# Straight writes and even-odd reads of PSUM in an induced attention and maxout kernel

## The chip, the cores and the metric

The kernel runs on one core of a Trainium2 chip. The metric is the device time of one execution in microseconds (us). The engines that matter are TensorE (PE in the profile, with its weight loads as PEld), ScalarE (ACT), VectorE (DVE) and GpSimd (POOL); SyncE (SP) issues nearly all DMAs. SBUF is the on-chip working memory, PSUM the memory that matmuls write; it has eight banks of 512 fp32 columns on each of 128 partitions.

## What is computed

```python
def mab(q, kv):
    s = scale * (q @ kv.transpose(0, 2, 1))
    s = s - s.max(-1, keepdims=True)
    a = np.exp(s)
    a /= a.sum(-1, keepdims=True) + 1e-09
    return a @ kv
h = mab(I, x)          # x: 4 x 12544 x 128, I: 32 inducing points per batch
x = mab(x, h)          # every token attends to the 32 rows of h
h = np.maximum(np.maximum(x @ w1, x @ w2), x @ w3)     # 128 -> 768
out = h @ w_out                                        # 768 -> 128
```

All is in fp32 to the accuracy of a split: a value is kept as a high part, rounded to the type fp32r in which a matmul runs at one pass, and a low part that holds the rest.

## The kernel before

A batch has 12544 tokens, cut into one narrow group of 256 tokens and six groups of 2048. A full group is worked in four chunks of 512 tokens; the narrow one is one chunk of 256. So a batch has 25 chunks and the whole has 100. Each chunk goes through six slots (`NJ = 6`, 128 of the 768 hidden columns each), 600 slots in all.

For a token the second attention gives 32 weights. The weights' high and low halves, each twice, fill the 128 rows of a tile `pT`, and the columns of `pT` are the chunk's tokens. The matrix `us` holds w1-w2, w3-w2 and a product through `w_out`, each already multiplied with the batch's attended points. With z = x w2 the maximum of three is z + max(relu(x(w1-w2)), x(w3-w2)), and z's own way through `w_out` is folded into the third part of `us`.

A slot does this, in `advance()` and, `LAG = 6` slots later, in `stage2()`:

- PE: a product into bank `pu` (line 787) and one into bank `pv` (line 797), both reading `pT`. There are two banks of each.
- ACT: `ru` = relu of `pu`, from PSUM to SBUF (line 806).
- DVE: `h` = maximum of `pv` in PSUM and `ru` in SBUF (line 827).
- ACT: `hi` = `h` rounded to fp32r (line 816), SBUF to SBUF.
- POOL, in some slots DVE: `lows` = `h` - `hi` (lines 824 and 830).
- PE: three products that add into bank `acc`: `wo_hi` with `hi`, `wo_lo` with `hi`, `wo_hi` with `lows` (lines 863 to 865). In a chunk's first slot a fourth goes ahead of them, the third part of `us` with `pT` (line 862).

After a chunk's sixth slot `finish()` copies `acc` to `o` in SBUF (line 876, on ACT but for the first three chunks and a half of the last) and stores it.

Once in a group of 24 slots `scores_steps()` makes the weights: products (line 692), transposes, exponentials and divisions in a PSUM bank `aux`, then ACT writes the high halves `ph` (line 739) and DVE the low halves `pl` (line 742). SP's DMAs move them row by row into the `pT` of four chunks (line 768), two chunks ahead of their use. The first attention of the next batch (lines 366 to 545) is put in between as single steps until the last batch, where nothing follows.

The order of everything is written out by hand: the slot loop in `main()` and a table of slots. Each engine does its list in that order.

A matmul's moving operand is not read column by column here. `woven` reads the two halves of 512 columns in turn: 0, 256, 1, 257 and so on. So the output's columns come in another order than the input's. Before the change this is made up for in SBUF: `ph` and `pl` are written scattered (`spread`), value 4b+2d+a of a row at column 256d+128a+b, so that each written value is 128 or more columns from the last. `pu`, `pv`, `ru`, `h`, `hi` and `lows` then hold the chunk in an order that a second reading by halves puts right, and `acc` and `o` come out straight. The product of line 862 makes one step where the others make two, so it reads `pT` by quarters in turn: 0, 128, 256, 384, 1 and so on. The narrow chunks (`full` is false) are read and written straight throughout.

```python
    def woven(ap, full):
        return ap.rearrange("p (a b) -> p b a", a=2) if full else ap
    def spread(ap, full):
        return ap.rearrange("p (d a b) -> p b d a", d=2, a=2) if full else ap
```

Of the kernel before, what the change touches and what calls it, by code (L numbers as in the profile page):

```python
# [8 lines left out]
F32 = mybir.dt.float32  # L9
# [3 lines left out]
AF = mybir.ActivationFunctionType  # L13
# [12 lines left out]
def kernel(ctx, tc, x, xt, ind_t, w1, w2, w3, w_out, out):  # L26
    nc = tc.nc
    B, N, C = x.shape
    M = ind_t.shape[1]
    DF = w1.shape[1]  # L30
    P = 128
    NT = N // P
    NJ = DF // P
# [158 lines left out]
    def first_load(what):  # L192
# [12 lines left out]
        out=sel[:, :M], in_=ident.rearrange("p (q m) -> p m q", m=M), axis=AX.X, op=ALU.add  # L205
    )
    nc.vector.tensor_copy(
        out=sel[:, M:].rearrange("p (q m) -> p q m", m=M),
        in_=sel[:, :M].unsqueeze(1).to_broadcast([P, NQ - 1, M]),
# [17 lines left out]
    wo_hi = const.tile([P, NJ, C], F32R, name="wo_hi")  # L227
    wo_lo = const.tile([P, NJ, C], F32R, name="wo_lo")
# [54 lines left out]
    def row_of(j):  # L283

        return 2 * (j % (NJ // 2)) + j // (NJ // 2)
# [388 lines left out]

    def woven(ap, full):

        return ap.rearrange("p (a b) -> p b a", a=2) if full else ap

    def spread(ap, full):

        return ap.rearrange("p (d a b) -> p b d a", d=2, a=2) if full else ap

    def scores_products(b, gi, bank):
        nt = groups[gi]["nt"]
# [10 lines left out]
    def scores_steps(b, gi):  # L697

        nt = groups[gi]["nt"]
        w = nt * M  # L700
        st = state[b]
        sp = st["s"].pop(gi)
        flat = sp[:, :w]
        ev = flat.rearrange("p (t m) -> p t m", m=M)
        nc.vector.transpose(out=flat, in_=flat)
        yield
        mx = wk.tile([P, GT], F32, name="mx", tag="mx")
        nc.vector.tensor_reduce(out=mx[:, :nt], in_=ev, axis=AX.X, op=ALU.max)
        yield
        nc.vector.tensor_sub(out=ev, in0=ev, in1=mx[:, :nt].unsqueeze(2).to_broadcast([P, nt, M]))  # L710
        yield
        nc.scalar.activation(out=flat, in_=flat, func=AF.Exp, scale=scale)
        yield
        rs = wk.tile([P, GT], F32, name="rs", tag="rs")
        nc.vector.tensor_reduce(out=rs[:, :nt], in_=ev, axis=AX.X, op=ALU.add)
        yield
        if b == 0 and gi < 2:
            nc.vector.tensor_scalar_add(out=rs[:, :nt], in0=rs[:, :nt], scalar1=1e-9)
        else:
            nc.scalar.activation(out=rs[:, :nt], in_=rs[:, :nt], func=AF.Identity, bias=eps)  # L720
        yield
        nc.vector.reciprocal(out=rs[:, :nt], in_=rs[:, :nt])
        nc.vector.tensor_mul(out=ev, in0=ev, in1=rs[:, :nt].unsqueeze(2).to_broadcast([P, nt, M]))
        yield
        if nt < GT:

            pn = wk.tile([P, nt, 2, 2, M], F32R, name="pn", tag="pn", bufs=1)
            e4 = ev.unsqueeze(2).to_broadcast([P, nt, 2, M])
            nc.scalar.copy(out=pn[:, :, :, 0, :], in_=e4)
            yield  # L730
            nc.vector.tensor_sub(out=pn[:, :, :, 1, :], in0=e4, in1=pn.bitcast(F32)[:, :, :, 0, :])
            st[("p", gi)] = pn
            yield
            return
        nc.vector.transpose(out=flat, in_=flat)  # L735
        yield
        e4 = flat.rearrange("p (b d a) -> p b d a", d=2, a=2)
        ph = wk.tile([P, 512], F32R, name="ph", tag="ph")
        nc.scalar.copy(out=spread(ph, True), in_=e4)  # L739
        yield  # L740
        pl = wk.tile([P, 512], F32R, name="pl", tag="pl")
        nc.vector.tensor_sub(out=spread(pl, True), in0=e4, in1=spread(ph.bitcast(F32), True))  # L742
        st[("p", gi)] = (ph.bitcast(F32), pl.bitcast(F32))
        yield

# [28 lines left out]
    relus, sums = {}, {}  # L774
# [5 lines left out]
    def advance():  # L780

        s = pipe["next"]
        pipe["next"] += 1
        if s + 1 < len(slots):
            c, j = slots[s + 1]
            pu, w = bank_u[(s + 1) % 2], c.w
            nc.tensor.matmul(  # L787
                out=pu[:, :w],
                lhsT=state[c.b]["us"][:, 2 * j * P : (2 * j + 1) * P],
                rhs=woven(c.pT[:, :w], c.full),  # L790
                start=True,
                stop=True,
            )
        if 0 <= s < len(slots):
            d, j = slots[s]
            pv = bank_v[s % 2]
            nc.tensor.matmul(  # L797
                out=pv[:, : d.w],
                lhsT=state[d.b]["us"][:, (2 * j + 1) * P : (2 * j + 2) * P],
                rhs=woven(d.pT[:, : d.w], d.full),  # L800
                start=True,
                stop=True,
            )
        if s + 1 < len(slots):
            ru = hp.tile([P, 512], F32, name="ru", tag="ru", bufs=3)
            nc.scalar.activation(out=ru[:, :w], in_=pu[:, :w], func=AF.Relu)  # L806
            relus[s + 1] = ru
        low = pipe.pop("low", None)
        if 0 <= s - 1 < len(slots):
            c, j = slots[s - 1]  # L810
            h = sums.pop(s - 1)
            hi = hp.tile([P, 512], F32R, name="hi", tag="hi", bufs=10)
            if s - 1 in HIVEC:
                nc.vector.tensor_copy(out=hi[:, : c.w], in_=h[:, : c.w])
            else:
                nc.scalar.copy(out=hi[:, : c.w], in_=h[:, : c.w])  # L816
            lo = lows[:, (s - 1) % NL, :]
            c.hh.append(hi)
            c.hl.append(lo)
            args = dict(out=lo[:, : c.w], in0=h[:, : c.w], in1=hi.bitcast(F32)[:, : c.w])  # L820
            if c.low(j):
                pipe["low"] = args
            else:
                nc.gpsimd.tensor_sub(**args)  # L824
        if 0 <= s < len(slots):
            h = hp.tile([P, 512], F32, name="h", tag="h", bufs=5)
            nc.vector.tensor_max(out=h[:, : d.w], in0=pv[:, : d.w], in1=relus.pop(s)[:, : d.w])  # L827
            sums[s] = h
        if low:
            nc.vector.tensor_sub(**low)  # L830

    class Chunk:


        def __init__(self, n, b, gi, q):
            self.n, self.b, self.gi, self.q = n, b, gi, q
            self.w = GT * M if q is not None else groups[gi]["nt"] * P
            self.full = q is not None
            self.hh, self.hl = [], []

        def low(self, k):
# [7 lines left out]
    def stage2(c, j):  # L849
        us = state[c.b]["us"]  # L850
        w = c.w
        hi, lo = (woven(t[:, :w], c.full) for t in (c.hh[j], c.hl[j]))
        if j == 0:
            c.acc = [(bank_o[c.n % 2], slice(0, w))]
            if c.n == len(chunks) - 1:
                c.acc = [(bank_a[k], slice(k * w // 2, (k + 1) * w // 2)) for k in range(2)]
        for acc, cs in c.acc:
            to = acc[:, : cs.stop - cs.start]
            two, four = (slice(cs.start // k, cs.stop // k) if c.full else cs for k in (2, 4))
            if j == 0:  # L860
                pT = spread(c.pT[:, :w], c.full)
                nc.tensor.matmul(out=to, lhsT=us[:, 2 * DF :], rhs=pT[:, four], start=True, stop=False)  # L862
            nc.tensor.matmul(out=to, lhsT=wo_hi[:, row_of(j), :], rhs=hi[:, two], start=False, stop=False)  # L863
            nc.tensor.matmul(out=to, lhsT=wo_lo[:, row_of(j), :], rhs=hi[:, two], start=False, stop=False)  # L864
            nc.tensor.matmul(out=to, lhsT=wo_hi[:, row_of(j), :], rhs=lo[:, two], start=False, stop=(j == NJ - 1))  # L865

    def finish(c):
        at = groups[c.gi]["at"] + (c.q or 0) * c.w
        turns = [(nc.vector.tensor_copy if c.n < 3 else nc.scalar.copy, nc.sync)]
        if len(c.acc) > 1:  # L870

            turns = [(nc.vector.tensor_copy, nc.sync), (nc.scalar.copy, nc.scalar)]
        for (acc, cs), (copy, queue) in zip(c.acc, turns):
            o = op.tile([P, 512], F32, name="o", tag="o", bufs=3)
            w = cs.stop - cs.start
            copy(out=o[:, :w], in_=acc[:, :w])  # L876
            queue.dma_start(out=out[c.b, :, at + cs.start : at + cs.stop], in_=o[:, :w])


# [7 lines left out]
    for b in range(B):  # L887
        for gi in range(NG):
            full = groups[gi]["nt"] == GT
# [41 lines left out]
    def begins(win):  # L931
        b, g = divmod(win - 1, NG - 1)
        return b * per_batch + short + g * WIN

    for win, slot, kind, n, gi in MOVES:
        s = begins(win) + slot
# [39 lines left out]
    for n, turns in enumerate(TURNS, start=1):  # L976
        for gi, win, slot, wait, past in turns:
            s = begins(win) + slot
# [9 lines left out]
        s = begins(win) + (8 if slot < 8 else 20)  # L988
# [164 lines left out]
```

## Time and profile before

| What | us |
|---|---|
| median of 3 runs | 800.47 (800.38 to 800.72) |
| the profiled execution | 799.86 |
| its span, first to last instruction | 798.1 |
| PE busy | 781.7 (98%) |
| ACT busy | 737.0 (92%) |
| DVE busy | 641.4 (80%) |
| POOL busy | 638.3 (80%) |

The first relu starts at 47 us; what lies ahead of it loads the inputs and runs the first batch's first attention. From there to 790 us the slots run. The granted TensorE clock is full (1.00) in every stretch. The busy time of PE is modelled, since matmuls overlap; how fast it really goes is read from the distance between the starts of one matmul and the next in the timeline. The same goes for ACT and DVE, where an instruction's record overlaps the next one's by some 0.1 to 0.3 us. The chain is the work that ended last, followed back from the end; a shorter instruction off the chain moves nothing by itself.

### The profile page before, as it was taken

What the parts mean: (1) busy time and instruction counts of PE and PEld (TensorE: products, weight loads), DVE (VectorE), ACT (ScalarE), POOL (GpSimd) and SP (SyncE); (2) the same over time, 40 slices, a digit from 0 to 9 for tenths busy, and PEclk for the clock granted to TensorE, in tenths of its full rate; (3) what the DMA queues carried; (4) which work ended last, traced back from release to release, by engine and by line L of the source; (5) the groups of instructions that cost most, each with busy time, mean ns of one, the idle gap of its engine ahead of it and who ended that gap; (6) DMA issues with size and microseconds to landing.
All of it is one profiled execution on the core that took longest, in us unless ns stands there. A gap on an engine that the chain in (4) does not pass through costs nothing.

```text
span 798.1 us, 14349 instructions
## 1 busy us (share of the span) xinstructions
PE 781.7 (98%) x4567; PEld 627.2 (79%) x4567; DVE 641.4 (80%) x1071; ACT 737.0 (92%) x1529; POOL 638.3 (80%) x523
## 2 busy tenths in 40 slices
PE   8999999999999999999999999999999999999998
PEld 6668878778788787787778877878878788787887
DVE  5898978778877787887886878878888788888875
ACT  5789899899998898998998999999999999999996
POOL 1379868878788797786887978878878888888887
PEclk9999999999999999999999999999999999999999
DMA  9844325274542643543644336334223222222221
GB/s 358 297 132 126 107 79 175 61 247 159 190 138 65 194 132 100 185 119 106 223 132 129 108 103 198 114 112 132 68 82 93 74 80 80 67 84 65 77 81 53
DMA packets 52266, 102.24 MB, mean 128 GB/s; under 512 B 18144, under 2 KB 21344, under 8 KB 46944
## 3 DMA queue, kind: packets, MB, share of 16 engines
q1 hardware_dynamic: 52048, 101.21, 40.3%
q8 instruction: 36, 0.59, 0.3%
q14 instruction: 38, 0.31, 0.1%
q10 hardware_dynamic: 144, 0.13, 0.0%
HBM read 48.12 MB, written 25.69 MB: 92 GB/s over the span
## 4 chain that ended last, share of the span: by engine, by line
ACT 44%; PE 43%; DMA 4%; POOL 3%; DVE 3%; issue 2%; SPq 1%; POOLq 0%; ACTq 0%; DVEq 0%
ACT ru L806 18%; ACT hi L816 18%; PE pu L787 7%; PE acc L863 7%; PE pv L797 7%; PE acc L864 6%; PE acc L865 6%; POOL lows L824 3%; ACT o L876 3%; PE aux L692 3%; DMA raw<-in_w_out_dram 2%; PE acc L502 2%; ACT ph L739 2%; PE aux L366 2%; PE acc L862 1%
## 5 line engine op out<-in xcount | busy, mean ns | idle before, releaser
L824 POOL TENSOR_TENSOR lows<-h,hi 128x512 fp32r<-128x512 f32 (+1 forms) x504 | 623.1, 1268 | 123.6 <-ACT hi L816 120.0
L827 DVE TENSOR_TENSOR h<-pv,ru 128x512 f32<-128x512 f32 (+1 forms) x600 | 400.5, 674 | 122.6 <-PE pv L797 57.1
L806 ACT ACTIVATE ru<-pu 128x512 f32<-128x512 f32 (+1 forms) x600 | 402.0, 671 | 36.9 <-PE pu L787 36.7
L816 ACT CAST hi<-h 128x512 fp32r<-128x512 f32 (+1 forms) x596 | 410.9, 690 | 0.8 <-DVE h L827 0.6
L787 PE MATMUL pu<-pT,us 128*128 128x512 f32 (+1 forms) x600 | 229.6, 383 | 6.5 <-ACT ru L806 5.9
L797 PE MATMUL pv<-pT,us 128*128 128x512 f32 (+1 forms) x600 | 226.3, 377 | 1.7 <-DVE h L827 1.6
L863 PE MATMUL acc<-hi,wo_hi 128*128 128x512 f32 (+1 forms) x594 | 225.9, 380 | 0.0
L865 PE MATMUL acc<-lows,wo_hi 128*128 128x512 f32 (+1 forms) x594 | 222.8, 375 | 0.0
L864 PE MATMUL acc<-hi,wo_lo 128*128 128x512 f32 (+1 forms) x594 | 222.8, 375 | 0.0
L787 PEld LDWEIGHTS pu<-pT,us 128*128 128x128 f32 x600 | 113.1, 188 | 40.3 <-ACT ru L806 22.7
L863 PEld LDWEIGHTS acc<-hi,wo_hi 128*128 128x128 f32 x594 | 112.2, 189 | 22.1 <-issue 7.5
L797 PEld LDWEIGHTS pv<-pT,us 128*128 128x128 f32 x600 | 113.3, 189 | 20.0 <-DVE h L827 5.2
L864 PEld LDWEIGHTS acc<-hi,wo_lo 128*128 128x128 f32 x594 | 112.4, 189 | 20.2
L865 PEld LDWEIGHTS acc<-lows,wo_hi 128*128 128x128 f32 x594 | 112.2, 189 | 15.3
L830 DVE TENSOR_TENSOR lows<-h,hi 128x512 fp32r<-128x512 f32 x96 | 80.6, 839 | 0.8 <-ACT hi L816 0.8
L876 ACT COPY o<-acc 128x512 f32<-128x512 f32 (+1 forms) x96 | 64.5, 672 | 0.0
L862 PE MATMUL acc<-pT,us 128*128 128x512 f32 (+1 forms) x99 | 43.0, 434 | 0.0
L742 DVE TENSOR_TENSOR pl<-aux,ph 128x512 fp32r<-128x512 f32 x24 | 25.9, 1078 | 13.5 <-ACT ph L739 13.5
L739 ACT CAST ph<-aux 128x512 fp32r<-128x512 f32 x24 | 28.1, 1171 | 0.2 <-DVE aux L735 0.2
L502 PEld LDWEIGHTS acc<-xg,aT 128*32 128x32 f32 x640 | 18.0, 110 | 9.7 <-issue 8.0
L692 PE MATMUL aux<-xT,hT 128*32 128x512 f32 x192 | 25.1, 603 | 0.0
L366 PE MATMUL aux<-xT,iT 128*32 128x512 f32 x184 | 24.1, 596 | 0.2 <-ACT pT L765 0.2
(163 smaller groups left out, 450.9 us busy)
## 6 DMA issues: line engine op xcount, KB each, us to landing
out_dram<-o SPq DMA_DIRECT2D x95, 256.0 KB, 2.2
xg<-in_x_dram SPq DMA_DIRECT2D x23, 1024.0 KB, 5.9
xT<-in_xt_dram SPq DMA_DIRECT2D x18, 1024.0 KB, 5.5
pT<-ph SPq DMA_DIRECT2D x190, 64.0 KB, 2.0
pT<-pl SPq DMA_DIRECT2D x190, 64.0 KB, 2.0
raw<-in_w_dram SPq DMA_DIRECT2D x3, 768.0 KB, 8.6
us<-uh SPq DMA_DIRECT2D x24, 52.0 KB, 1.9
us<-ul SPq DMA_DIRECT2D x24, 52.0 KB, 2.6
```

The source lines that it names most:

```text
L787: nc.tensor.matmul(out=pu[:, :w], lhsT=state[c.b]["us"][:, 2 * j * P : (2 * j + 1) * P], rhs=woven(c.pT[:, :w], c.full), start=True, stop= ...
L797: nc.tensor.matmul(out=pv[:, : d.w], lhsT=state[d.b]["us"][:, (2 * j + 1) * P : (2 * j + 2) * P], rhs=woven(d.pT[:, : d.w], d.full), start ...
L806: nc.scalar.activation(out=ru[:, :w], in_=pu[:, :w], func=AF.Relu)
L816: nc.scalar.copy(out=hi[:, : c.w], in_=h[:, : c.w])
L824: nc.gpsimd.tensor_sub(**args)
L827: nc.vector.tensor_max(out=h[:, : d.w], in0=pv[:, : d.w], in1=relus.pop(s)[:, : d.w])
L830: nc.vector.tensor_sub(**low)
L862: nc.tensor.matmul(out=to, lhsT=us[:, 2 * DF :], rhs=pT[:, four], start=True, stop=False)
L863: nc.tensor.matmul(out=to, lhsT=wo_hi[:, row_of(j), :], rhs=hi[:, two], start=False, stop=False)
L864: nc.tensor.matmul(out=to, lhsT=wo_lo[:, row_of(j), :], rhs=hi[:, two], start=False, stop=False)
L865: nc.tensor.matmul(out=to, lhsT=wo_hi[:, row_of(j), :], rhs=lo[:, two], start=False, stop=(j == NJ - 1))
L876: copy(out=o[:, :w], in_=acc[:, :w])
```

## The change

The scattered writes go and the reads of PSUM take their place.

- Every product of `pT`, `hi` and `lows`, that of line 862 and those of the narrow chunks too, reads halves in turn (`turned`).
- `ph` and `pl` are written straight.
- A product's output in PSUM then holds token 256a+b at column 2b+a. The relu, the maximum and the output copy read their PSUM bank by even columns first and odd columns after (`sorted_`, every second fp32, twice 256 of them) and write straight (`halves` only gives the straight side the same shape). `ru`, `h`, `hi`, `lows` and `o` are all in the tokens' order.

Each engine has the same instructions in the same order as before; only access patterns differ.

```diff
-    def woven(ap, full):
-        return ap.rearrange("p (a b) -> p b a", a=2) if full else ap
-    def spread(ap, full):
-        return ap.rearrange("p (d a b) -> p b d a", d=2, a=2) if full else ap
+    def turned(ap):
+        return ap.rearrange("p (a b) -> p b a", a=2)
+    def sorted_(ap):
+        return ap.rearrange("p (b a) -> p a b", a=2)
+    def halves(ap):
+        return ap.rearrange("p (a b) -> p a b", a=2)
...
-        e4 = flat.rearrange("p (b d a) -> p b d a", d=2, a=2)
         ph = wk.tile([P, 512], F32R, name="ph", tag="ph")
-        nc.scalar.copy(out=spread(ph, True), in_=e4)
+        nc.scalar.copy(out=ph, in_=flat)
         yield
         pl = wk.tile([P, 512], F32R, name="pl", tag="pl")
-        nc.vector.tensor_sub(out=spread(pl, True), in0=e4, in1=spread(ph.bitcast(F32), True))
+        nc.vector.tensor_sub(out=pl, in0=flat, in1=ph.bitcast(F32))
...
-                rhs=woven(c.pT[:, :w], c.full),
+                rhs=turned(c.pT[:, :w]),
...
-                rhs=woven(d.pT[:, : d.w], d.full),
+                rhs=turned(d.pT[:, : d.w]),
...
-            nc.scalar.activation(out=ru[:, :w], in_=pu[:, :w], func=AF.Relu)
+            nc.scalar.activation(out=halves(ru[:, :w]), in_=sorted_(pu[:, :w]), func=AF.Relu)
...
-            nc.vector.tensor_max(out=h[:, : d.w], in0=pv[:, : d.w], in1=relus.pop(s)[:, : d.w])
+            nc.vector.tensor_max(out=halves(h[:, : d.w]), in0=sorted_(pv[:, : d.w]), in1=halves(relus.pop(s)[:, : d.w]))
...
-        hi, lo = (woven(t[:, :w], c.full) for t in (c.hh[j], c.hl[j]))
...
-                pT = spread(c.pT[:, :w], c.full)
-                nc.tensor.matmul(out=to, lhsT=us[:, 2 * DF :], rhs=pT[:, four], start=True, stop=False)
-            nc.tensor.matmul(out=to, lhsT=wo_hi[:, row_of(j), :], rhs=hi[:, two], start=False, stop=False)
-            nc.tensor.matmul(out=to, lhsT=wo_lo[:, row_of(j), :], rhs=hi[:, two], start=False, stop=False)
-            nc.tensor.matmul(out=to, lhsT=wo_hi[:, row_of(j), :], rhs=lo[:, two], start=False, stop=(j == NJ - 1))
+                nc.tensor.matmul(out=to, lhsT=us[:, 2 * DF :], rhs=turned(c.pT[:, cs]), start=True, stop=False)
+            nc.tensor.matmul(out=to, lhsT=wo_hi[:, row_of(j), :], rhs=turned(c.hh[j][:, cs]), start=False, stop=False)
+            nc.tensor.matmul(out=to, lhsT=wo_lo[:, row_of(j), :], rhs=turned(c.hh[j][:, cs]), start=False, stop=False)
+            nc.tensor.matmul(out=to, lhsT=wo_hi[:, row_of(j), :], rhs=turned(c.hl[j][:, cs]), start=False, stop=(j == NJ - 1))
...
-            copy(out=o[:, :w], in_=acc[:, :w])
+            copy(out=halves(o[:, :w]), in_=sorted_(acc[:, :w]))
```

## Rows read from the trace of the kernel before

**Rows 1.** The page: busy time, share of the span and instructions of each engine.

```profile
PE 781.7 (98%) x4567; PEld 627.2 (79%) x4567; DVE 641.4 (80%) x1071; ACT 737.0 (92%) x1529; POOL 638.3 (80%) x523
```

**Rows 2.** Busy time by stretch: start, end, length, then PE, PEld, DVE, ACT, POOL.

```profile
0.00:48.00 48.00, 43.24 (x468) 29.61 (x469) 34.96 (x72) 33.28 (x79) 15.17 (x19) 1.00 0.85 316
...
442.00:562.00 120.00, 118.10 (x666) 94.38 (x666) 96.95 (x156) 112.89 (x231) 98.55 (x79) 1.00 0.43 131
...
772.00:798.00 26.00, 22.78 (x122) 20.03 (x120) 16.36 (x22) 19.73 (x39) 21.39 (x16) 1.00 0.18 61
```

**Rows 3.** The page: the chain that ended last, by engine and by line.

```profile
ACT 44%; PE 43%; DMA 4%; POOL 3%; DVE 3%; issue 2%; SPq 1%; POOLq 0%; ACTq 0%; DVEq 0%
ACT ru L806 18%; ACT hi L816 18%; PE pu L787 7%; PE acc L863 7%; PE pv L797 7%; PE acc L864 6%; PE acc L865 6%; POOL lows L824 3%; ACT o L876 3%; PE aux L692 3%; DMA raw<-in_w_out_dram 2%; PE acc L502 2%; ACT ph L739 2%; PE aux L366 2%; PE acc L862 1%
```

**Rows 4.** Timeline of ACT, two pieces: start, length, instruction.

```profile
385.56 0.72 ACT L816 CAST hi<-h 128x512 fp32r<-128x512 f32 x1
386.07 1.19 ACT L739 CAST ph<-aux 128x512 fp32r<-128x512 f32 x1
386.94 0.74 ACT L806 ACTIVATE ru<-pu 128x512 f32<-128x512 f32 x1
387.47 0.72 ACT L816 CAST hi<-h 128x512 fp32r<-128x512 f32 x1
...
390.96 0.73 ACT L876 COPY o<-acc 128x512 f32<-128x512 f32 x1
391.44 0.75 ACT L806 ACTIVATE ru<-pu 128x512 f32<-128x512 f32 x1
```

**Rows 5.** Timeline of PE beside it; idle time and its releaser in brackets.

```profile
387.05 0.38 PE L865 MATMUL acc<-lows,wo_hi 128*128 128x512 f32 x1
387.74 0.48 PE L787 MATMUL pu<-pT,us 128*128 128x512 f32 x1 [0.31 <-ACT ru L806]
...
389.14 0.38 PE L797 MATMUL pv<-pT,us 128*128 128x512 f32 x1
389.36 0.44 PE L862 MATMUL acc<-pT,us 128*128 128x512 f32 x1
389.63 0.38 PE L863 MATMUL acc<-hi,wo_hi 128*128 128x512 f32 x1
```

**Rows 6.** Timeline of PE, two products of a narrow chunk and the next.

```profile
236.46 0.28 PE L787 MATMUL pu<-pT,us 128*128 128x256 f32 x1
236.58 0.28 PE L797 MATMUL pv<-pT,us 128*128 128x256 f32 x1
236.70 0.44 PE L862 MATMUL acc<-pT,us 128*128 128x512 f32 x1
```

**Rows 7.** Instruction groups, shapes apart: count, busy us, mean ns, idle before.

```profile
L806 ACT ACTIVATE ru<-pu 128x512 f32<-128x512 f32 x576 | 391.8, 680 | 36.3 <-PE pu L787 36.1
L876 ACT COPY o<-acc 128x512 f32<-128x512 f32 x93 | 63.3, 680 | 0.0
L739 ACT CAST ph<-aux 128x512 fp32r<-128x512 f32 x24 | 28.1, 1171 | 0.2 <-DVE aux L735 0.2
L827 DVE TENSOR_TENSOR h<-pv,ru 128x512 f32<-128x512 f32 x576 | 390.9, 685 | 118.5 <-PE pv L797 55.7 <-ACT ru L806 25.9 <-POOL lows L824 14.9
L742 DVE TENSOR_TENSOR pl<-aux,ph 128x512 fp32r<-128x512 f32 x24 | 25.9, 1078 | 13.5 <-ACT ph L739 13.5
L862 PE MATMUL acc<-pT,us 128*128 128x512 f32 x95 | 41.8, 440 | 0.0
```

**Rows 8.** The same view: start-up instructions, L256 and L262 reading every second word of SBUF.

```profile
L256 DVE SCALAR_TENSOR_TENSOR rest<-raw,pw 128x768 f32<-128x768 uint32 x4 | 3.8, 959 | 0.1
L264 DVE TENSOR_TENSOR rest<-rest,t 128x768 f32<-128x768 f32 x1 | 0.9, 948 | 0.0
L262 ACT ACTIVATE size<-raw 128x768 f32<-128x768 f32 x4 | 3.7, 951 | 0.0
L311 ACT CAST wo_hi<-wf 128x768 fp32r<-128x768 f32 x1 | 0.8, 831 | 2.9 <-DVE wf L273 2.9
```

More of the change, by code (lines that the diff above doesn't have):

```diff
@@ L837, in __init__ @@
             self.w = GT * M if q is not None else groups[gi]["nt"] * P
-            self.full = q is not None
             self.hh, self.hl = [], []
@@ L858, in stage2 @@
             to = acc[:, : cs.stop - cs.start]
-            two, four = (slice(cs.start // k, cs.stop // k) if c.full else cs for k in (2, 4))
             if j == 0:
-                pT = spread(c.pT[:, :w], c.full)
-                nc.tensor.matmul(out=to, lhsT=us[:, 2 * DF :], rhs=pT[:, four], start=True, stop=False)
-            nc.tensor.matmul(out=to, lhsT=wo_hi[:, row_of(j), :], rhs=hi[:, two], start=False, stop=False)
-            nc.tensor.matmul(out=to, lhsT=wo_lo[:, row_of(j), :], rhs=hi[:, two], start=False, stop=False)
-            nc.tensor.matmul(out=to, lhsT=wo_hi[:, row_of(j), :], rhs=lo[:, two], start=False, stop=(j == NJ - 1))
+                nc.tensor.matmul(out=to, lhsT=us[:, 2 * DF :], rhs=turned(c.pT[:, cs]), start=True, stop=False)
+            nc.tensor.matmul(out=to, lhsT=wo_hi[:, row_of(j), :], rhs=turned(c.hh[j][:, cs]), start=False, stop=False)
+            nc.tensor.matmul(out=to, lhsT=wo_lo[:, row_of(j), :], rhs=turned(c.hh[j][:, cs]), start=False, stop=False)
+            nc.tensor.matmul(out=to, lhsT=wo_hi[:, row_of(j), :], rhs=turned(c.hl[j][:, cs]), start=False, stop=(j == NJ - 1))
     def finish(c):
```

## The prediction

> **What bounds the kernel now.** I read the busy line first: PE is busy for 98% of the span, ACT for 92%, DVE and POOL for 80% [rows 1]. Alone this says TensorE is the bound. The chain says otherwise: ACT holds 44% of it and PE 43% [rows 3]. The two take turns, and the timeline shows how. A wide matmul follows the last one after 0.22 us (389.14 to 389.36), so a slot's five take 1.08 to 1.10 us [rows 5]. On ACT a relu costs about 0.5 us from start to start (386.94 to 387.47, with the scattered cast still draining ahead of it), an output copy 0.48 us (390.96 to 391.44), the cast of `h` 0.51 us (385.56 to 386.07) [rows 4]; so relu and cast take 1.0 us of a slot, and one output copy in six slots adds another 0.08 us per slot. That is as much as PE's share, before ACT's work for softmax and first attention. Where that work falls, PE waits: at 387.74 a `pu` product comes 0.69 us after the start of the one ahead of it instead of 0.22, released by a relu [rows 5]. In 442 to 562 us ACT is busy for 112.9 of 120 us and PE for 118.1 [rows 2]. So a saving on either engine counts only in its turns, and a cost on ACT, which reads PSUM 696 times for relu and output, counts at once.
>
> **The change, part by part.** Instructions, order, DMAs and waits stay as they were; no instruction is queued behind a new wait. All that can move is how long single instructions take.
>
> *The cast `ph`* is written straight. The scattered one takes 0.87 us from its start to the next one's (386.07 to 386.94); a straight copy out of PSUM takes 0.48 us [rows 4]. That is 0.39 us off each of 24 [rows 7], 9.4 us of ACT in all. The chain holds 2% of 798.1 us, 16.0 us, in this line [rows 3]; 45% of it (0.39 of 0.87) goes: 7.2 us. What is late next is PE, and at the place shown PE had lost 0.69 - 0.22 = 0.47 us, so 0.39 us can be had there before PE is the bound again.
>
> *The subtraction `pl`* falls from 1078 to about the 685 ns of a maximum that also reads one operand in PSUM and one in SBUF [rows 7]: 0.39 us times 24, 9.4 us of DVE. DVE has 20% idle time [rows 1] and 3% of the chain [rows 3], and `pl` feeds DMAs two chunks ahead of their use. I count it at nothing; the idle time of DVE is what hides it, and nothing would be lost if that went, since the term is a saving.
>
> *The fourth product* (line 862) reads halves where it read quarters: from 0.27 us to the next start (389.36 to 389.63) to the 0.22 of its neighbours [rows 5], 0.055 us with the rounding spread over five starts. For 95 of them [rows 7] PE saves 5.2 us. The chain holds 1%, 8.0 us, in this line [rows 3], of which a fifth goes: 1.6 us.
>
> *The narrow chunks* read halves where they read straight. A product of 256 columns takes 0.12 us now [rows 6]; half of a wide one that reads by halves is 0.11 us [rows 5]. With 5 products in each of 24 narrow slots this is 0 to 1.2 us; I take nothing.
>
> *The reads of PSUM by every second column* are the unknown: 576 wide relus and 93 wide copies on ACT, 576 wide maxima on DVE [rows 7], and 27 narrow ones on ACT and 24 on DVE of half the length. No row of the trace shows a stepped read of PSUM. A gain is excluded, since as many elements are read as before. The nearest rows are stepped reads of SBUF. On DVE, line 256 reads every second word and takes 959 ns, against 948 for a straight operation of the same size [rows 8]: no cost. On ACT, line 262 reads every second word and takes 951 ns against 831 for a straight cast [rows 8]: 120 ns on 768 elements, 80 ns on 512, if the function is not to blame. The far row is the scattered write of `ph`: 1171 against 680 ns for a straight copy [rows 7], 491 ns. So the price of one ACT read lies between 0 and 0.49 us. I take 0, for this reason: a relu's source is a bank that by the order of the program no other engine touches at the time, and the DVE row shows that a step of two words by itself need not cost. The choice is the weak point of this prediction, and both ends stay in the cases below.
>
> [...]
>
> *The sum* at a price of 0: 7.2 + 1.6 = 8.8 us off the chain. Part of it will not be had, since with ACT's turns shorter PE's path ends last in places where it now ends just ahead; I take off a fifth and say 7 us. Made against the profiled execution that is 799.86 - 7 = 792.9 us; the median of the runs lies 0.6 us above it, so the forecast is 793 us. Its own range: 799 if only the relief of a few groups shows, 787 if all 24 casts (9.4 us) and most of PE's savings land on the path.
>
> **The rivals.**
>
> *A small price on ACT.* The chain holds 18% + 3% = 21% of 798 us in relu and output copy [rows 3], 168 us, or about 345 of the 696 at 0.485 us each [rows 4]. So 8.8 us are eaten by 25 ns per read: from there on the change loses. At 20 to 30 ns the result is no change that can be told. At the 80 ns of line 262 the 345 on the chain cost 28 us, and all 696 cost 55 us if ACT becomes the bound throughout: 819 to 846 us, 832 in the middle. For it: ACT is as full as PE. Against it: line 262 differs in function and ran while the inputs poured in (first 48 us).
>
> *A large price on ACT*, the slower side in full. Each read pays like the scattered write, 0.49 us: 669 wide ones and 27 of half that are 335 us. ACT is then busy for 737 - 9 + 335 = 1063 us, and with the 21 us that it idles before 48 and after 772 us [rows 2] the time is about 1085 us. PE would wait for `pu` banks in every slot. For it: reads and writes of SBUF that land on a fresh place each time do cost this much in this trace (`ph`, `pl`). Against it: those jump 128 columns and more, this steps over one.
>
> [...]
>
> *A large price on DVE alone.* The 393 ns by which `pl` exceeds a maximum [rows 7], on 576 wide and 24 narrow maxima, is 231 us. DVE would be busy for 641 - 9 + 231 = 863 us, with 23 us of idle time at the two ends [rows 2] some 885 us. DVE idles for 157 us, 134 of them in the slots' stretch; with the 9 us from `pl` that is 0.24 us per maximum before DVE decides.
>
> *That the change does not do what it says*: the straight `ph` still costs 0.87 us because its target, not its order, is slow. Then only 1.6 us remain, 799. The straight output copies from the same kind of bank at 0.48 us speak against it.
>
> **How the numbers follow.** No price, 793 us with 787 to 799: 0.57. No change that can be measured (a price of 20 to 30 ns, or a cast that stays slow), 799 to 802: 0.08. A small price, 802 to 850: 0.17. A large price on ACT, around 1085: 0.13. A large price on DVE, around 885: 0.05. Leaving out the last two leaves 0.18 out, so the range is 787 to 850; the price of 0.49 us at its end is outside it and is told here. About 0.2%, 1.6 us, is what a measurement of this kernel can tell from no change. Faster 0.57, same 0.08, slower 0.35.
>
> **What would show it.** In the profile after: the wide relu, output copy and maximum at 680, 680 and 685 ns as before (any rise is the price, to be multiplied as above); `ph` at 680 and `pl` at about 690 ns; the fourth product at 0.22 us to the next start; the narrow products at 0.11. Then the chain should hold less of ACT and more of PE, and the wait of `pu` products for relus should be smaller. The prediction is wrong if relu and copy take over 25 ns longer. It is also wrong, in the other direction, if the kernel gains over 13 us, since that is more than the two engines' savings can be worth in turn.

## The result, and the profile after

The changed kernel takes 790.47 us (median of 4 runs, 790.24 to 790.76) against 800.45 us before: a ratio of 0.9875, 95% interval 0.9858 to 0.9892, or 10.0 us. The prediction was 793 us, in a range of 787 to 850. The profiled execution took 790.35 us with a span of 788.5 us.

The page of the changed kernel: busy time, then the chain by engine and by line.

```profile
PE 774.7 (98%) x4567; PEld 626.4 (79%) x4567; DVE 639.4 (81%) x1071; ACT 727.1 (92%) x1529; POOL 639.6 (81%) x523
...
PE 56%; ACT 33%; POOL 3%; DMA 3%; DVE 2%; issue 1%; SPq 0%; POOLq 0%; ACTq 0%; DVEq 0%
ACT ru L809 14%; ACT hi L819 13%; PE pu L790 10%; PE acc L862 9%; PE pv L800 9%; PE acc L863 9%; PE acc L864 9%; PE aux L696 3%; POOL lows L827 3%; ACT o L875 2%; PE acc L502 2%; DMA raw<-in_w_dram 2%; PE aux L366 2%; PE acc L861 2%; ACT aux L449 1%
```

ACT had 44% of the chain and PE 43% [rows 3]; now PE leads with 56% to 33%. The cast `ph`, 2% before, is gone from the list.

The groups of the changed kernel with shapes apart, the counterparts of [rows 7] (count, busy us, mean ns, idle before):

```profile
L809 ACT ACTIVATE ru<-pu 128x512 f32<-128x512 f32 x576 | 396.3, 688 | 37.1 <-PE pu L790 36.9
L875 ACT COPY o<-acc 128x512 f32<-128x512 f32 x93 | 64.1, 689 | 0.0
L742 ACT CAST ph<-aux 128x512 fp32r<-128x512 f32 x24 | 16.1, 672 | 0.2 <-DVE aux L739 0.2
...
L830 DVE TENSOR_TENSOR h<-pv,ru 128x512 f32<-128x512 f32 x576 | 391.2, 683 | 119.6 <-PE pv L800 60.0 <-ACT ru L809 27.3 <-POOL lows L827 15.2
...
L745 DVE TENSOR_TENSOR pl<-aux,ph 128x512 fp32r<-128x512 f32 x24 | 16.5, 689 | 4.4 <-ACT ph L742 3.8 <-DMA xT<-in_xt_dram 0.5
```

The maximum, which now reads PSUM by even and odd columns, takes 683 ns (685 before). `ph` fell from 1171 to 672 ns and `pl` from 1078 to 689. Relu and output copy rose from 680 to 688 and 689 ns, which the first group of experiments looks into.

Timeline of ACT in the changed kernel, the counterpart of [rows 4]:

```profile
508.36 0.70 ACT L809 ACTIVATE ru<-pu 128x512 f32<-128x512 f32 x1
508.85 0.71 ACT L819 CAST hi<-h 128x512 fp32r<-128x512 f32 x1
509.36 0.69 ACT L742 CAST ph<-aux 128x512 fp32r<-128x512 f32 x1
509.84 0.71 ACT L809 ACTIVATE ru<-pu 128x512 f32<-128x512 f32 x1
510.33 0.73 ACT L819 CAST hi<-h 128x512 fp32r<-128x512 f32 x1
```

From start to start a relu takes 0.49 us (508.36 to 508.85) and `ph` 0.48 (509.36 to 509.84), where it took 0.87.

Timeline of PE beside it, and at a fourth product, the counterpart of [rows 5]:

```profile
510.36 0.38 PE L864 MATMUL acc<-lows,wo_hi 128*128 128x512 f32 x1
510.61 0.48 PE L790 MATMUL pu<-pT,us 128*128 128x512 f32 x1
510.93 0.38 PE L800 MATMUL pv<-pT,us 128*128 128x512 f32 x1
...
63.33 0.38 PE L800 MATMUL pv<-pT,us 128*128 128x512 f32 x1
63.55 0.38 PE L861 MATMUL acc<-pT,us 128*128 128x512 f32 x1
63.76 0.38 PE L862 MATMUL acc<-hi,wo_hi 128*128 128x512 f32 x1
```

The `pu` product behind `ph`, which came 0.69 us after the matmul ahead of it, now comes after 0.25; with 0.22 for an unhindered one, the stall went from 0.47 to 0.03 us. The fourth product is followed after 0.21 us instead of 0.27.

The product behind such a late one comes after 0.32 us (510.61 to 510.93), another 0.10 us late, and it did so in the kernel before (from 387.74, in [rows 5]):

```profile
388.06 0.38 PE L797 MATMUL pv<-pT,us 128*128 128x512 f32 x1
```

### The profile page after: what moved, and what is told of

It is laid out like the page before. It is cut to its first block, busy times and chain, and to the rows that moved or that the text cites. A ratio compares the mean times of both kernels' runs of the same rounds, so it can differ in the third digit from the quotient of the medians.

```text
span 788.5 us, 14348 instructions
## 1 busy us (share of the span) xinstructions
PE 774.7 (98%) x4567; PEld 626.4 (79%) x4567; DVE 639.4 (81%) x1071; ACT 727.1 (92%) x1529; POOL 639.6 (81%) x523
## 4 chain that ended last, share of the span: by engine, by line
PE 56%; ACT 33%; POOL 3%; DMA 3%; DVE 2%; issue 1%; SPq 0%; POOLq 0%; ACTq 0%; DVEq 0%
ACT ru L809 14%; ACT hi L819 13%; PE pu L790 10%; PE acc L862 9%; PE pv L800 9%; PE acc L863 9%; PE acc L864 9%; PE aux L696 3%; POOL lows L827 3%; ACT o L875 2%; PE acc L502 2%; DMA raw<-in_w_dram 2%; PE aux L366 2%; PE acc L861 2%; ACT aux L449 1%
## 5 line engine op out<-in xcount | busy, mean ns | idle before, releaser
L809 ACT ACTIVATE ru<-pu 128x512 f32<-128x512 f32 (+1 forms) x600 | 407.0, 679 | 37.8 <-PE pu L790 37.5
L819 ACT CAST hi<-h 128x512 fp32r<-128x512 f32 (+1 forms) x596 | 416.3, 699 | 0.3 <-DVE h L830 0.2
L833 DVE TENSOR_TENSOR lows<-h,hi 128x512 fp32r<-128x512 f32 x96 | 87.7, 913 | 0.8 <-ACT hi L819 0.8
L861 PE MATMUL acc<-pT,us 128*128 128x512 f32 (+1 forms) x99 | 37.3, 376 | 0.0
L502 PE MATMUL acc<-xg,aT 128*32 128x128 f32 x640 | 21.4, 273 | 0.1
L861 PEld LDWEIGHTS acc<-pT,us 128*128 128x128 f32 x99 | 18.7, 189 | 2.6 <-DVE hs L540 0.2
```

Source lines behind the costliest of these rows:

```text
L809: nc.scalar.activation(out=halves(ru[:, :w]), in_=sorted_(pu[:, :w]), func=AF.Relu)
L861: nc.tensor.matmul(out=to, lhsT=us[:, 2 * DF :], rhs=turned(c.pT[:, cs]), start=True, stop=False)
```

## The experiments

All are edits of the changed kernel. Three chips were used. The kernel before took 800.48 us on the first (straight reads, cast, subtraction, quarters), 799.88 on the second (steps of four and sixteen, all straight, narrow chunks) and 800.29 on the third (the versions meant to be faster), so times from different chips can be compared to within about 0.6 us.

### Is a read of every second column free?

```diff
-nc.scalar.activation(out=halves(ru[:, :w]), in_=sorted_(pu[:, :w]), func=AF.Relu)
+nc.scalar.activation(out=ru[:, :w], in_=pu[:, :w], func=AF.Relu)
...   (the maximum and the output copy likewise)
```

> The changed kernel with relu, maximum and output copy reading their PSUM bank straight; each chunk's tokens are left in the order in which the products put them. If a read of every second column has no price: 790.5 us, within 0.6, and relu, copy and maximum from start to next start as in the changed kernel. Rival: the mean of a wide relu rose from 680 to 688 ns and that of the copy from 680 to 689; if this is a price of 8 ns, the 260 or so on the chain give back 2 us: 788.4.

Measured: 790.32 us (790.17 to 790.40). Steps of four and of sixteen columns, in the same three places:

```diff
-        return ap.rearrange("p (b a) -> p a b", a=2)
+        return ap.rearrange("p (b a) -> p a b", a=4)
...
-        return ap.rearrange("p (a b) -> p a b", a=2)
+        return ap.rearrange("p (a b) -> p a b", a=4)
```

> The changed kernel with relu, maximum and output copy reading every fourth column of their PSUM bank (four passes of 128) instead of every second; each chunk's tokens come out in another order. If a step in a PSUM read has no price at all: 790.5 us, within 0.6. Rival: the step of two is free only because it is short; with a step of 16 bytes each read pays some of what the scattered SBUF write paid (up to 0.39 us from start to start), which over 696 ACT reads is up to 270 us: 800 to 1060.

> As the kernel with every fourth column, but every sixteenth (16 passes of 32 columns). No price for a step: 790.5 us, within 1. Rival: a price that sets in with the length of the step or the number of passes, 800 us and more, read off the relu's distance from start to start.

Measured: 789.90 us (789.54 to 790.17) and 790.28 us (789.64 to 791.56). The groups of the wide relu and maximum, first with straight reads, then every fourth column, then every sixteenth:

```profile
L809 ACT ACTIVATE ru<-pu 128x512 f32<-128x512 f32 x576 | 395.4, 687 | 37.3 <-PE pu L790 37.1
L830 DVE TENSOR_TENSOR h<-pv,ru 128x512 f32<-128x512 f32 x576 | 391.2, 683 | 119.5 <-PE pv L800 60.4 <-ACT ru L809 27.5 <-POOL lows L827 15.0
```

```profile
L809 ACT ACTIVATE ru<-pu 128x512 f32<-128x512 f32 x576 | 394.0, 684 | 37.2 <-PE pu L790 37.0
L830 DVE TENSOR_TENSOR h<-pv,ru 128x512 f32<-128x512 f32 x576 | 391.7, 684 | 119.3 <-PE pv L800 60.0 <-ACT ru L809 26.5 <-POOL lows L827 15.6
```

```profile
L809 ACT ACTIVATE ru<-pu 128x512 f32<-128x512 f32 x576 | 394.6, 685 | 37.2 <-PE pu L790 37.0
L830 DVE TENSOR_TENSOR h<-pv,ru 128x512 f32<-128x512 f32 x576 | 391.6, 684 | 119.1 <-PE pv L800 60.4 <-ACT ru L809 26.5 <-POOL lows L827 15.6
```

A relu takes 687 ns with straight reads and 688 with those by every second column, so the 8 ns over the kernel before are no price of the step. The cast `hi`, which reads SBUF and was not edited, rose by as much, from 699 to 707 ns. And where no wait lies between, a wide relu takes 0.488 us from start to start on average over the changed kernel's timeline, 0.489 in the kernel before and 0.487 to 0.488 with the other steps. Of the steps that were run (1, 2, 4 and 16 columns) none has a price on either engine.

### What each of the removed costs was worth

The cast `ph` written scattered again:

```diff
-        nc.scalar.copy(out=ph, in_=flat)
+        nc.scalar.copy(out=spread(ph), in_=four(flat))
```

> The changed kernel (790.5 us) with ACT's cast ph written scattered again and nothing else; the columns of pT then stand in another order than the products assume, so the output's tokens are permuted. By the chain shares of the prediction (16.0 us of ph on the chain, 45% of it) the time rises by 7.2 us to 797.7. Rival: PE, which now holds 56% of the chain, covers the cast, and the ten us came mostly from PE's own savings (5.2 for the fourth product, up to 1.2 for the narrow chunks); then the rise is 3.5 us or less, to 794 at most.

Measured: 797.37 us (797.31 to 797.64), 6.9 us more. In its timeline, ACT and then PE around one `ph`:

```profile
98.99 1.20 ACT L750 CAST ph<-aux 128x512 fp32r<-128x512 f32 x1
99.86 0.75 ACT L817 ACTIVATE ru<-pu 128x512 f32<-128x512 f32 x1
```

```profile
99.84 0.38 PE L872 MATMUL acc<-lows,wo_hi 128*128 128x512 f32 x1
100.67 0.48 PE L798 MATMUL pu<-pT,us 128*128 128x512 f32 x1 [0.45 <-ACT ru L817]
100.99 0.38 PE L808 MATMUL pv<-pT,us 128*128 128x512 f32 x1
```

The 0.87 us from start to start are back, and so is the stall: the `pu` product comes 0.83 us after the one ahead of it. Adding up, over the groups, what this product is late against 0.216 us gives 7.4 us in 16 groups here, 1.0 us in the changed kernel and 5.9 us in the kernel before. So 6.4 of the 6.9 us are lost at this one place.

The subtraction `pl` scattered again (reads of `ph` and writes of `pl`):

```diff
-        nc.vector.tensor_sub(out=pl, in0=flat, in1=ph.bitcast(F32))
+        nc.vector.tensor_sub(out=spread(pl), in0=four(flat), in1=spread(ph.bitcast(F32)))
```

> The changed kernel with DVE's subtraction pl reading ph and writing pl scattered again and nothing else; the low halves then belong to other tokens than the high ones, so the output is not the reference's. The prediction counted pl at nothing: 790.5 us, within 1 us. Rival: the maximum queued behind pl on DVE is late by 0.39 us in each of 24 groups and hands that on to the casts and to PE: up to 9.4 us more, 800.

Measured: 790.73 us (790.53 to 791.24), 0.3 us more, which is within the spread of the runs. DVE's 9 us are covered by its idle time, as counted.

The fourth product by quarters again:

```diff
-rhs=turned(c.pT[:, cs]), start=True, stop=False)
+rhs=(spread(c.pT)[:, slice(cs.start // 4, cs.stop // 4)] if c.q is not None else turned(c.pT[:, cs])), start=True, stop=False)
```

> The changed kernel with the product of line 861 reading pT by quarters in turn again and nothing else; that third part of the sum then goes to permuted tokens. By chain share in the profile before: 1.6 us more, 792.1. Rival: since PE holds 56% of the chain after the change, more than half of the 95 x 0.055 = 5.2 us comes back: 793.5 to 795.7.

Measured: 792.10 us (791.88 to 792.34), 1.6 us more. Of the 5.2 us that PE saves, less than a third shows. That PE's part of the chain is larger after the change does not raise it. The timeline says where the rest goes: against 0.216 us from start to start, PE loses 5.6 us behind the fourth products here and 0.1 in the changed kernel, but its `pu` products are late by 6.3 us in all instead of 8.0, and the `pv` products behind them by 5.4 instead of 7.0. A PE that comes later finds more relus done.

The narrow chunks straight again:

```diff
     def turned(ap):
-        return ap.rearrange("p (a b) -> p b a", a=2)
+        return ap.rearrange("p (a b) -> p b a", a=2) if ap.shape[1] == 512 else ap
...   (sorted_ and halves likewise)
```

> The changed kernel with the four narrow chunks read straight again, products and PSUM reads; the result is the reference's. The prediction allowed 0 to 1.2 us and took nothing. Casts (6.9), subtraction (0.3) and fourth product (1.6) have now given 8.8 of the 10.0 us, so that 1.2 us are left for this: 791.7. Rival: the narrow products lie beside other work and the rest is an interaction of the other three: 790.5.

Measured: 790.88 us (790.61 to 792.52), on the chip on which the steps of four and sixteen took 789.90 and 790.28: 0.6 to 1.0 us more. The groups of the narrow `pu` product, with narrow chunks straight and then in the changed kernel:

```profile
L790 PE MATMUL pu<-pT,us 128*128 128x256 f32 x24 | 7.0, 294 | 0.0
```

```profile
L790 PE MATMUL pu<-pT,us 128*128 128x256 f32 x24 | 6.7, 285 | 0.0
```

The record of a `pu` product is 9 ns shorter by halves, those of the others 6 to 8, and there are 124 narrow ones: 1.1 us at most. The direction is as expected, but the runs spread over more than the effect, so the size is not settled.

### What do the reads by halves buy at all?

```diff
     def turned(ap):
-        return ap.rearrange("p (a b) -> p b a", a=2)
+        return ap
...   (and the PSUM reads straight, as in the first experiment)
```

> The changed kernel with every product reading straight and every PSUM read straight; the result is the reference's. What do the reads by halves buy? From the narrow products, which take 0.12 us straight and 0.11 by halves: 13 ns for each wide one, five a slot, 576 wide slots: 37 us of PE; at PE's 56% of the chain 21 us, and all of it if PE becomes the bound throughout: 811 to 828. Rival: straight wide reads are as fast as those by halves and the narrow ones lose for another reason: 790.

Measured: 808.97 us (808.59 to 809.32); the ratio to the kernel before is 1.0114 (1.0097 to 1.0131). Its timeline of PE and its chain by engine:

```profile
300.14 0.39 PE L800 MATMUL pv<-pT,us 128*128 128x512 f32 x1
300.37 0.39 PE L862 MATMUL acc<-hi,wo_hi 128*128 128x512 f32 x1
300.60 0.39 PE L863 MATMUL acc<-hi,wo_lo 128*128 128x512 f32 x1
300.82 0.39 PE L864 MATMUL acc<-lows,wo_hi 128*128 128x512 f32 x1
```

```profile
PE 96%; DMA 2%; DVE 1%; ACT 0%; issue 0%; SPq 0%; ACTq 0%; DVEq 0%
```

A straight wide product is followed after 0.227 us (0.68 for three), one by halves after 0.216: 11 ns, not the 13 worked out from the narrow ones, which is why 809 lies just below the range that was expected. With 2880 such products in the wide slots that is 32 us of PE, and PE now ends everything; of the 32 us, 18.5 show, since the stalls behind ACT vanish: what the wide slots' products are late against an unhindered distance falls from 18.9 to 6.7 us, 12.2 of the other 13.5.

### A version meant to be faster

After the change PE still waits for a relu at one place in 12 groups, behind an output copy and the first attention's exponential on ACT. The attempt gives a cast `hi` per group to DVE.

```diff
-            if s - 1 in HIVEC:
+            if s - 1 in HIVEC or (c.q is not None and s > 20 and NJ * c.q + j == 20):
```

> The changed kernel itself once more, on the chip of the next three: 790.5 us.

> A version meant to be faster. In the changed kernel's timeline PE waits for a relu in slot 23 of 12 of the 24 groups, 0.47 us each, 5.6 us in all, since ACT has an output copy and the first attention's exponential there; the stall at the cast ph has all but gone. Here the cast hi of slot 20 of every group is made by DVE instead, which has 19% idle time: ACT reaches slot 23 some 0.5 us earlier. If ACT's backlog is the cause: 785 to 787. Rival: the cast on DVE delays the maximum queued behind it by about 0.4 us and the stall only moves to the maximum, or DVE's cast and POOL's subtractions slow each other: 790 or more.

> As n1, with the cast hi of slot 13 on DVE too, ahead of ph. The stalls left at slots 16 and 18 are 1.3 and 1.0 us in all, so at best 2 us below n1: 783 to 785. Rival: DVE does softmax work around slot 13 and its maximum comes late: no better than n1, or worse.

> As n1, but not in the last batch, which has no first attention and no stall at slot 23: the same as n1 within 0.6 us if the gain is that stall alone; slower than n1 if the last batch gains too, faster if n1's casts on DVE cost there.

Measured: the changed kernel 789.79 us (789.68 to 789.91), ratio 0.9862 (0.9846 to 0.9878). One cast on DVE 796.78 us (792.34 to 797.47), two 800.10 us (797.37 to 803.75), one without the last batch 794.87 us (794.38 to 796.03). All are slower than the changed kernel; the one with two casts is no faster than the kernel before. The last is the easiest to read. From its timeline, DVE and POOL, then PE, then the busy times and the granted clock (after the POOL column) of 79.4 to 82.4 us:

```profile
74.38 4.37 DVE L817 CAST hi<-h 128x512 fp32r<-128x512 f32 x1
78.66 1.27 DVE L830 TENSOR_TENSOR h<-pv,ru 128x512 f32<-128x512 f32 x2
```

```profile
69.79 8.67 POOL L827 TENSOR_TENSOR lows<-h,hi 128x512 fp32r<-128x512 f32 x7
78.82 3.75 POOL L827 TENSOR_TENSOR lows<-h,hi 128x512 fp32r<-128x512 f32 x3 [0.36 <-DVE hi L817]
```

```profile
75.48 0.38 PE L790 MATMUL pu<-pT,us 128*128 128x512 f32 x1
79.40 0.77 PE L800 MATMUL pv<-pT,us 128*128 128x512 f32 x1 [3.54 <-DVE h L830]
79.97 0.63 PE L862 MATMUL acc<-hi,wo_hi 128*128 128x512 f32 x1
80.39 0.63 PE L863 MATMUL acc<-hi,wo_lo 128*128 128x512 f32 x1
...
82.10 0.63 PE L861 MATMUL acc<-pT,us 128*128 128x512 f32 x1
82.53 0.55 PE L862 MATMUL acc<-hi,wo_hi 128*128 128x512 f32 x1
```

```profile
79.40:82.40 3.00, 3.00 (x7) 2.44 (x8) 1.29 (x3) 2.76 (x6) 3.00 (x3) 0.51 0.00 0
```

One cast, in the first full group, took 4.37 us: it began while POOL worked through seven queued subtractions without a pause and ended 0.29 us after the last of them. The other 18 wide casts on DVE in this version began while POOL ran no subtraction, and took 0.41 to 0.43 us. The maximum queued behind it on DVE came late, the `pv` product waited for its bank, and PE lost 3.92 - 0.22 = 3.7 us. Then its granted clock was 0.51 of full, and the seven matmuls from 79.40 on took 3.13 us to the next one's start instead of 1.5: 1.6 us more. Together that is 5.3 us, and the measured loss against the changed kernel is 5.1 us. The same cast takes 4.37 to 4.38 us in all three versions. So in this one the other casts together gained next to nothing. What came is the rival named beforehand as far as the cast goes, long beside the subtractions, with the maximum late; the seven subtractions themselves were not slowed (8.67 us, 1.24 each, against a mean of 1.30 in the changed kernel).

PE's waits (total us, times, longest) in the changed kernel, in the version without the last batch, and in that with two casts:

```profile
PE pu L790 <- ACT ru L809: 3.7, 12, 0.3
PE pv L800 <- DVE h L830: 1.5, 3, 0.7
```

```profile
PE pv L800 <- DVE h L830: 5.0, 4, 3.5
PE pu L790 <- ACT ru L809: 3.6, 12, 0.3
```

```profile
PE pv L800 <- DVE h L830: 14.9, 24, 3.5
```

With one cast on DVE, PE's wait for relus stays: the half microsecond that ACT was given did not reach the place where PE waits, and why not was not followed further. With two casts no wait of a `pu` product for a relu is on the list, but the waits for maxima grow from 1.5 to 14.9 us. There the long cast is no matter of the first group: the casts of slot 13 took 0.8 to 3.0 us in 20 of 23 groups. No version was tried that moves a later cast and spares the first group, and what the casts of the last batch cost (796.78 against 794.87 us) was not followed.

## Why the prediction was right

*The unknown, the price of a stepped read of PSUM,* was taken at 0 out of a span of 0 to 0.49 us. It is 0 on both engines: a relu takes 688 ns at every second column and 687 straight, a maximum 683 and 683. The weak row was that of line 262 (80 ns on ACT from reading every second word of SBUF); whatever lengthened it, reads of PSUM do not have it, and the same instruction, not edited, takes 995 ns in the changed kernel, so the row was a loose bound. The reason that was given, that a step by itself need not cost, is borne out for the steps that were run; for ACT it was carried over from a row of DVE reading SBUF, so there the right choice was in part luck. Whether it matters that no other engine touches the bank was not tested. The rivals of a price, small or large, on either engine fall.

*The terms of the sum* came out one by one. The cast: 7.2 us forecast, 6.9 measured, through the very stall that the timeline had shown. The subtraction: nothing forecast, 0.3 measured. The fourth product: 1.6 forecast, 1.6 measured, of 5.2 us of PE's time. The share of the chain times the fraction that goes was a better measure in each case than the busy time. That it fits to a few tenths is luck: a share printed as 2% lies between 1.5 and 2.5%, 5.4 to 9.0 us for the cast, and one printed as 1% gives 0.8 to 2.4 us for the product. With the pieces of the chain added up one by one, some 17.2 and 11.4 us, the terms would have been 7.7 and 2.3 us.

*The size* was 3 us short (7 us forecast off the chain, 10.0 measured): 1.8 of it by the deduction, the rest by the two terms that were taken at nothing. The step that failed is the deduction: a fifth was taken off 8.8 us because PE's path was thought to end last in places where it ended just ahead. The runs show no such loss: 6.9 + 0.3 + 1.6 = 8.8 us came back when the three were undone one at a time. Another pair agrees: from the kernel before to the changed kernel with quarters 8.4 us go (800.48 to 792.10), and without the subtraction and the narrow chunks 7.1 to 7.5 of them are left for the cast. The prediction had read at one place that PE had lost 0.47 us, more than the 0.39 that go. That place is among the larger: at ten of the 16 the `pu` product was late by only 0.28 to 0.33 us. What the prediction did not count is the 0.10 us that PE loses once more behind each late product; with it 0.38 us and more could be had at 15 of the 16.

*The narrow chunks* were taken at nothing in a span of 0 to 1.2 us. With them straight again 0.6 to 1.0 us are lost, a size that the spread of those runs leaves open. Together the four account for 9.4 to 9.8 of the 10.0 us.

*The signs that were named* are in the profile: unchanged maximum, `ph` at 672 and `pl` at 689 ns, 0.21 us behind the fourth product, narrow products at 0.11, PE ahead of ACT on the chain. Relu and copy are the exception, 8 and 9 ns longer; any rise was to count as the price, and the straight reads show that this one is none.

## What to carry to other kernels

Where two engines take turns on the chain, work out each saving as its line's time on the chain (from its pieces, since the page rounds the shares) times the fraction that goes; add the terms, and take something off only where the timeline shows, place by place, that the other engine is right behind. A permutation that some pass has to undo is best put where it is free, and here that was the read of PSUM (a relu's 688 ns for 687), while the scattered write to SBUF cost nearly double (0.87 us for 0.48). Before work is moved to an engine with idle time on average, look at what the neighbouring engines do at that moment: one cast that took 4.37 us beside POOL's subtractions, instead of 0.42, cost more than the move could gain in one version, and in another the moved casts were long in 20 of 23 groups.

## What the runs showed of the hardware

- ACT's relu and DVE's maximum read 512 fp32 columns of PSUM by every second, fourth or sixteenth column in the time of a straight read (684 to 688 ns against 687, and 683 to 684 against 683).
- ACT's cast of 512 columns from PSUM to SBUF takes 0.87 us from start to start when it writes every element 128 or more columns from the last, and 0.48 when it writes straight.
- A `pu` product that came late behind a relu, by 0.03 us or by 0.61, is followed after 0.32 us instead of 0.22 (510.61 and 100.67). Why was not tested.
- A wide fp32r matmul is followed after 0.216 us when it reads SBUF by halves in turn, after 0.227 when it reads straight, and after 0.27 when it reads by quarters in turn.
- A DVE cast from SBUF to SBUF took 0.41 to 0.43 us in the 18 cases that began with POOL at no subtraction. The one that began within a run of seven POOL subtractions without a gap took 4.37 us and ended 0.3 us after the last of them. What held it up was not tested by a run of its own.
- After 3.9 us in which PE started no matmul its granted clock was 0.51 of full over the next 3 us (79.40 to 82.40).
